# Expert tiles of a fused attention and mixture-of-experts kernel: turned through DRAM by VectorE, with lists of 64-byte entries that each tile gathers itself

## Chip, core and metric

The kernel runs on one core of a Trainium2 chip. The metric is the device time of one execution in microseconds; the figure of a kernel is the median of its runs.

## What is computed

```
scores = z @ z.T / S              # B = 8 batches, S = 2496, z: S x 64
x = u * (relu(scores)**2 @ v)     # u, v: S x 256; 8 * 2496 = 19968 tokens
logits = x @ w_gate               # 256 x 8
e = argmax(logits)                # one expert per token
gate = softmax(logits)[e]
out = gate * (relu(x @ w1[e]) @ w2[e])   # w1: 256 x 1024, w2: 1024 x 256
```

Everything is float32. The kernel gets that accuracy by splitting each operand of a matmul in a high part (rounded to fp32r) and a low part (the rest), and by adding up three products.

## The kernel before

**Attention.** 8 batches of 5 chunks of up to 512 queries, each chunk in 10 steps of 256 keys: 400 steps. `scores` makes a block of squared scores (two matmuls per 128 keys into `ps_s`, Relu and Square on ScalarE, high part `thi`, low part `tlo`); where the block mirrored across the diagonal is there already, it is brought instead: `turn` (L241) transposes 32 x 32 blocks on VectorE and stores 1 MB to the DRAM tile `scr`, and `bring` (L253) reads it back with four DMAs that exchange the blocks. `weighted` (L298) multiplies with v into `acc`. `ready` holds the scores of three steps ahead. SyncE issues all these loads and stores in one queue, in order.

**After each chunk** `gate_x` (L323) makes x of the chunk, transposed, and puts three things in lists of background work, of which one is done in each step: `logits`; `turn_rows`, which writes x as token rows to the DRAM tensor `xrows` (L350); and `route` (L374): choose the expert, then `place`, which counts the token's place in its expert's list with small matmuls. `place` writes the gate beside the row (`xrows` has 272 floats a row: 256 of x, 16 of `gw` whose first is the gate; L429, L431), and scatters the token number, 4 bytes, to its place in the DRAM tensor `lst` by up to four indirect DMAs on GpSimd (L434, 128 tokens each). Unused places of `lst` hold the number of an empty row; `constants` (L205) fills them at the start with six DMAs from GpSimd (L218).

**Expert tiles.** `tile_list` (L444) works out, from the counts, which expert and which part of its list each tile gets: once for six tiles after the seventh batch (list A), and once for the rest after the eighth (list F). It gathers the lists of all tiles in two DMAs (L590), one tile per partition, and `places` (L597) transposes them on TensorE into `idx`, one token per partition. There are 47 tiles in the common path: 31 of four blocks of 128 tokens, 4 of three, 12 of two, mixed so that the two-block tiles are spread out. Two neighbouring tiles can share their weights.

The loop `tiles` (L898) runs over groups, eight in a tile (four in a two-block tile). In a group: `up` (L714) of the group two ahead (matmuls into `ph`, then the high part on ScalarE, L732, and the low part on VectorE, L733), and `down` (L737), which adds into `y`. Around them, at fixed groups:

- first group: `load_w` of the next weights (1 MB each, GpSimd, L639) and `load_x(i + 3)`, one indirect DMA per block, from `xrows` into `rows` (ring of three, L648);
- middle group: `turn_x(i + 2)` (L674). It copies the gates out (L679), cuts the 32-bit values in two 16-bit halves (L689; one half on ScalarE, one on VectorE) into a buffer of the ring `th` (three buffers of 128 x 4 KB), and SyncE transposes each block by a DMA into a second buffer of that ring (L692);
- third group from the end: `split_x(i + 1)` (L695), which joins the halves (L708 on ScalarE, L709 on VectorE) and makes the high part (L710) and the low part (L711). `pinned` (L313) holds it behind what was issued before on each engine;
- `split_piece` (L652) splits a quarter of the weights, two pieces ahead;
- last group: `finish` (L753), which scales with the gate on ScalarE (L760) and VectorE (L761) and scatters the rows to the output on GpSimd (L763).

The first tile is turned differently: copied at `turn_x(0)` (L683) and transposed on TensorE in `split_x(0)` (L704). In the last steps of attention a table `loads` names what is issued for the first tiles: at so many steps before the end `load_x(0)`, `load_w`, `turn_x(0)` and so on; `split_x(0)` stands at the step before the last.

The order of instructions on each engine is made by a scheduler from a model of times; it may put an instruction ahead of others of its engine as soon as its inputs and a buffer are there in that model. It also picks the buffer of a ring. Each engine then executes its own queue in that order.

Of the kernel before, what the change touches and what calls it, by code (L numbers as in the profile page):

```python
# [19 lines left out]
P = 128  # L20
KQ = 64
G, R = 4, 32
D = 256
# [3 lines left out]
ROW = 272  # L27
# [21 lines left out]
def fused_kernel(ctx: ExitStack, tc: tile.TileContext, zt, ut, v, wg, wcat, out):  # L49
# [43 lines left out]
    def ring_rows():  # L93
        return sb.tile([P, QC // P, ROW], F32, name="rows", tag="rows", bufs=3)

# [10 lines left out]
    xrows = dram.tile([NTOK + 1, ROW], F32, name="xrows")  # L106
    lst = dram.tile([NROW + 1, SMALL], F32, name="lst")
# [76 lines left out]
    def iota_i(name, pattern, base=0, mult=0):  # L184
        n = 1
        for _, c in pattern:
# [9 lines left out]
             iota_i("toks", [[S, B], [QC, NC_], [P, QC // P]], mult=1),  # L196
             iota_i("base0", [[CAP, E]]),
             iota_i("pcol", [[0, 1]], mult=2),
             iota_i("tno", [[1, NMAX]])]
    e_down, e_up, toks, base0, pcol, tno = [f for _, f in iotas]  # L200
    base = const.tile([P, E], F32, name="base")
    pads = sb.tile([P, 2, QC], F32, name="x", tag="x")
    padrow, fill = pads[0:1, 0, 0:ROW], pads[:, 1, 0:SMALL]

    def constants():  # L205
# [8 lines left out]
        nc.vector.memset(fill, float(NTOK))  # L214
        nc.gpsimd.dma_start(xrows[NTOK:NTOK + 1, :], padrow)
        for r in range(0, NROW + 1, P):
            m = min(P, NROW + 1 - r)
            nc.gpsimd.dma_start(lst[r:r + m, :], fill[:m])  # L218
# [104 lines left out]
    def gate_x(b, c, acc):  # L323
# [12 lines left out]
        gw = sb.tile([P, QC // P, ROW - D], F32, name="gw", bufs=3)  # L336
        nc.gpsimd.memset(gw, 0.0)
        lw = sb.tile([P, QC // P, R], F32, name="lw", bufs=2)
# [32 lines left out]
    scatters = []  # L371
    lst1 = lst.rearrange("a b -> (a b)").unsqueeze(1)

    def route(t0, n, ns, lw, gw):  # L374

        mlast = n - (ns - 1) * P
        col = (t0 // S * NC_ + t0 % S // QC) * (QC // P)
# [26 lines left out]
        def place():  # L404
# [22 lines left out]
            nf = n // P  # L427
            if nf:
                nc.sync.dma_start(xrows[t0:t0 + nf * P, D:].rearrange("(s p) r -> p s r", p=P), gw[:, 0:nf, :])  # L429
            if mlast < P:  # L430
                nc.sync.dma_start(xrows[t0 + nf * P:t0 + n, D:], gw[:mlast, nf, :])  # L431
            for j in range(ns):
                m = min(P, n - j * P)
                i = nc.gpsimd.indirect_dma_start(  # L434
                    out=lst1, out_offset=bass.IndirectOffsetOnAxis(ap=posi[:m, j:j + 1], axis=0),
                    in_=toks[:m, col + j:col + j + 1], in_offset=None)
                for o in scatters:
                    tc.declare_no_dep(i.ins, o.ins, reason="places are distinct")
                scatters.append(i)
# [4 lines left out]
    def tile_list(nm, nd, nb, n3, ns, done):  # L444
# [6 lines left out]
        kept = ("ndbl", "widx", "idx")  # L451
# [36 lines left out]
        lidx = t("lidx", (P, 2), I32)  # L488
        r["widx"] = t("widx", (P, 2, NT), I32)
        r["idx"] = t("idx", (P, BIG // P, NT), I32)  # L490
# [76 lines left out]
        def rows():  # L567
# [14 lines left out]
            nc.vector.tensor_tensor(lrow, lrow, ident[:, 0:NT], op=ALU.mult)  # L582
            lcol = t("lcol", (P, 1))
            nc.vector.tensor_reduce(lcol, lrow, axis=AX.X, op=ALU.add)
            nc.vector.tensor_copy(lidx[:, 0:1], lcol)
            nc.vector.tensor_scalar(lidx[:, 1:2], lcol, 1.0, float(NROW), op0=ALU.add, op1=ALU.min)
            for h in range(2):
                n = NT if h == 0 else NT - ns
                r["tl", h] = ring_raw().rearrange("p a d -> p (a d)")[:, 0:SMALL]
                nc.gpsimd.indirect_dma_start(out=r["tl", h][:n], out_offset=None, in_=lst,  # L590
                                             in_offset=bass.IndirectOffsetOnAxis(ap=lidx[:n, h:h + 1], axis=0))
# [5 lines left out]
        def places(h):  # L597
            n = NT if h == 0 else NT - ns
            pt = psm.tile([P, QC], F32, name="plt", tag="psm")
            for s in range(SMALL // P):  # L600
                nc.tensor.transpose(pt[:, s * NT:s * NT + n], r["tl", h][:n, s * P:(s + 1) * P], ident[:n, :n])
            for s in range(SMALL // P):
                nc.vector.tensor_copy(r["idx"][:, h * (SMALL // P) + s, 0:n], pt[:, s * NT:s * NT + n])

        return r, [count] + ([middle, others] if ns else []) + [experts, rows] + [nothing] * (6 if ns else 2) + [lambda: places(0), lambda: places(1)]
# [26 lines left out]
    lists, xgs, pieces, turned, gates, xts, yts = {}, {}, {}, {}, {}, {}, {}  # L632
# [9 lines left out]

    def load_x(i):
        which, t, k = order[i]
        src = xrows[0:NTOK - S, :] if which == "A" else xrows
        xg = ring_rows()
        for s in range(k):
            nc.gpsimd.indirect_dma_start(out=xg[:, s, :], out_offset=None, in_=src,  # L648
                                         in_offset=bass.IndirectOffsetOnAxis(ap=lists[which]["idx"][:, s, t:t + 1], axis=0))
        xgs[i] = xg  # L650
# [23 lines left out]
    def turn_x(i):  # L674
# [3 lines left out]
        gates[i] = sb.tile([P, BS], F32, name="gt", bufs=4)  # L678
        nc.vector.tensor_copy(gates[i][:, 0:k], xg[:, 0:k, D])  # L679
        if i == 0:  # L680
            flat = ring_halves().rearrange("p a n -> p (a n)").bitcast(F32)
            turned[i] = flat.rearrange("p (s e) -> p s e", e=D)
            nc.scalar.copy(turned[i].rearrange("p s (i g d) -> p s i g d", i=2, g=G),  # L683
# [132 lines left out]
    for b in range(B):  # L816
        for c in range(NC_):
            s0 = (b * NC_ + c) * NKP
            at(s0 + 2, lambda b=b, c=c: fetch_u(b, c))
            if b == 0:  # L820
                continue
# [161 lines left out]
```

## Time and profile before

| | |
|---|---|
| median of three runs | 2436.0 us (2424.96 to 2438.99) |
| the profiled execution's own time | 2426.16 us |
| its span | 2424.4 us |
| TensorE (PE) busy | 2274.0 us, 94% |
| VectorE (DVE) busy | 1657.8 us, 68% |
| ScalarE (ACT) busy | 1449.8 us, 60% |
| GpSimd (POOL) busy | 635.3 us, 26% |
| mean granted TensorE clock | 0.971 |
| moved by DMA | 383.08 MB, mean 158 GB/s |

How to read the profile: L12 is line 12 of the kernel. PE is the matmuls, PEld the weight loads that overlap them. Names of tiles stand as out<-in, and a `q` behind an engine means its queue alone (waiting or issuing). "Idle before" is the time in which the engine did nothing just before an instruction, and the name behind the arrow is what ended it. The windows view gives busy time in a stretch; the clock in it is the share of full speed that TensorE was granted. The waits view adds up idle time by who waited for whom. Times of DMAs run from issue to landing.

### The profile page before, as it was taken

The numbers are of one execution on the slowest core, as the hardware profiler recorded it, in microseconds if no ns is written. First come the engines' busy times: TensorE is split into PE (matmuls) and PEld (weight loads), VectorE is DVE, ScalarE is ACT, GpSimd is POOL, SyncE is SP. The second block draws the span as 40 slices with busy tenths as digits, with TensorE's granted clock in tenths as the row PEclk, the third lists the DMA queues.
The fourth block names the chain that finished last, engine by engine and source line by source line (L and its number), as shares of the span: only waits on it lengthen the run. The fifth ranks groups of instructions, "written<-read, shape, count | busy, mean of one in ns | idle before, by whom it ended". The sixth has DMA issues, their size and how long they took to land.

```text
span 2424.4 us, 31066 instructions
## 1 busy us (share of the span) xinstructions
PE 2274.0 (94%) x10880; PEld 1886.5 (78%) x10880; DVE 1657.8 (68%) x2895; ACT 1449.8 (60%) x1911; POOL 635.3 (26%) x637
## 2 busy tenths in 40 slices
PE   7999999999989999999999889886988998999998
PEld 4788878887877887878788778775877886888887
DVE  6877878878868878778787666453565564656554
ACT  5758658667657667576586444443554564646554
POOL 3110120120210200201221435433343443345422
PEclk8999999999999999999999989988999998999999
DMA  5777888878988688897787956646364556446430
GB/s 192 183 168 190 170 152 215 161 151 240 142 140 235 138 181 205 135 217 168 161 166 175 219 104 155 128 120 123 108 167 112 172 138 164 117 138 195 146 101 27
DMA packets 305492, 383.08 MB, mean 158 GB/s; under 512 B 209004, under 2 KB 211066, under 8 KB 285872
## 3 DMA queue, kind: packets, MB, share of 16 engines
q1 hardware_dynamic: 273936, 261.93, 51.3%
q0 software_dynamic: 31392, 119.10, 17.2%
q8 instruction: 87, 1.43, 0.3%
q14 instruction: 77, 0.63, 0.1%
HBM read 233.67 MB, written 127.32 MB: 149 GB/s over the span
## 4 chain that ended last, share of the span: by engine, by line
PE 62%; DMA 18%; DVE 7%; SPq 5%; ACT 5%; issue 3%; POOL 1%; ACTq 0%; DVEq 0%; POOLq 0%
PE ph L728 12%; PE acc L309 10%; PE acc L306 10%; PE acc L308 10%; PE y L749 9%; DMA scr<-s 8%; DMA th<-th 6%; PE y L751 4%; PE ps_s L280 3%; PE ps_s L281 3%; DMA s<-scr 3%; SPq L692 2%; SPq L258 2%; DVE t L733 1%; PE pt L357 1%
## 5 line engine op out<-in xcount | busy, mean ns | idle before, releaser
L306 PE MATMUL acc<-thi,t 128*128 128x512 f32 (+1 forms) x1200 | 457.0, 392 | 29.2 <-ACT thi L272 17.7
L309 PE MATMUL acc<-thi,t 128*128 128x512 f32 (+1 forms) x1200 | 464.9, 390 | 1.6 <-POOL t L145 1.6
L308 PE MATMUL acc<-tlo,t 128*128 128x512 f32 (+1 forms) x1144 | 448.5, 392 | 16.3 <-DVE tlo L287 10.3
L749 PE MATMUL y<-t,t 128*128 128x512 f32 x1062 | 389.9, 407 | 47.9 <-ACT t L732 34.4
L728 PE MATMUL ph<-thi,t 128*128 128x512 f32 (+2 forms) x1248 | 378.3, 365 | 15.4 <-DVE t L733 11.1
L282 ACT ACTIVATE tf<-ps_s 128x1024 f32<-128x1024 f32 (+1 forms) x240 | 242.2, 1017 | 220.1 <-PE ps_s L281 211.1
L732 ACT ACTIVATE t<-ph 128x512 fp32r<-128x512 f32 (+1 forms) x328 | 191.8, 589 | 248.6 <-PE ph L728 206.9
L733 DVE SCALAR_TENSOR_TENSOR t<-ph,t 128x512 fp32r<-128x512 f32 (+1 forms) x328 | 219.6, 673 | 176.3 <-ACT t L732 174.7
L751 PE MATMUL y<-t,t 128*128 128x256 f32 x1062 | 293.5, 286 | 5.5 <-DVE t L733 5.3
L306 PEld LDWEIGHTS acc<-thi,t 128*128 128x128 f32 x1200 | 227.5, 190 | 79.4 <-ACT thi L272 21.0
L434 POOL DMA_INDIRECT lst<-toks,posi x160 | 187.3, 1171 | 382.6 <-DMA xrows<-gw 223.9
L749 PEld LDWEIGHTS y<-t,t 128*128 128x128 f32 x1062 | 203.3, 194 | 92.5 <-ACT t L732 36.1
L728 PEld LDWEIGHTS ph<-thi,t 128*128 128x128 f32 x1248 | 227.0, 191 | 56.8 <-DVE t L733 15.3
L308 PEld LDWEIGHTS acc<-tlo,t 128*128 128x128 f32 x1144 | 218.3, 191 | 62.6 <-DVE tlo L287 13.6
L309 PEld LDWEIGHTS acc<-thi,t 128*128 128x128 f32 x1200 | 228.7, 191 | 44.9 <-POOL t L145 3.3
L283 ACT ACTIVATE tf<-tf 128x1024 f32<-128x1024 f32 (+1 forms) x240 | 250.4, 1053 | 4.6
L287 DVE TENSOR_TENSOR tlo<-tf,thi 128x1024 fp32r<-128x1024 f32 (+1 forms) x168 | 203.4, 1214 | 48.0 <-ACT thi L285 47.0
L728 PE MATMUL ph<-tlo,t 128*128 128x512 f32 (+2 forms) x624 | 227.1, 365 | 6.6 <-DVE tlo L711 6.6
L248 DVE STREAM_TRANSPOSE s<-tf 128x1024 f32<-128x1024 f32 x160 | 197.3, 1234 | 48.1 <-ACT tf L283 48.1
L763 POOL DMA_INDIRECT out_dram<-tf,lfidx x136 | 148.3, 1091 | 299.8 <-DVE tf L761 272.7
L751 PEld LDWEIGHTS y<-t,t 128*128 128x128 f32 x1062 | 206.6, 195 | 19.0 <-DVE t L733 8.0
L272 ACT CAST thi<-s 128x1024 fp32r<-128x1024 f32 x104 | 108.7, 1048 | 144.8 <-DMA s<-scr 70.0
(250 smaller groups left out, 4107.4 us busy)
## 6 DMA issues: line engine op xcount, KB each, us to landing
scr<-s SPq DMA_DIRECT2D x80, 1024.0 KB, 8.7
s<-scr SPq DMA_DIRECT2D x320, 256.0 KB, 6.2
vr<-in_v_dram SPq DMA_DIRECT2D x80, 256.0 KB, 6.5
u<-in_ut_dram SPq DMA_DIRECT2D x32, 512.0 KB, 6.4
xrows<-th SPq DMA_DIRECT2D x128, 128.0 KB, 9.4
zr<-in_zt_dram SPq DMA_DIRECT2D x36, 256.0 KB, 6.2
u<-in_ut_dram SPq DMA_DIRECT2D x8, 448.0 KB, 7.0
xrows<-th SPq DMA_DIRECT2D x32, 112.0 KB, 6.8
```

The lines of the kernel that those rows point to most:

```text
L248: nc.vector.transpose(out=to, in_=a.rearrange("p i (t s k) -> p i t s k", t=4, s=G))
L282: nc.scalar.activation(a[:, :, :n], ps[:, :, :n], AF.Relu)
L283: nc.scalar.activation(a[:, :, :n], a[:, :, :n], AF.Square)
L287: nc.vector.tensor_tensor(lo[:, :, :n], a[:, :, :n], hi[:, :, :n].bitcast(F32), op=ALU.subtract)
L306: nc.tensor.matmul(acc[d][:, :n], lhsT=vh, rhs=hi[:, i, :n], start=first and i == 0, stop=False)
L308: nc.tensor.matmul(acc[d][:, :n], lhsT=vh, rhs=lo[:, i, :n], start=False, stop=False)
L309: nc.tensor.matmul(acc[d][:, :n], lhsT=vl, rhs=hi[:, i, :n], start=False, stop=last and i == 1)
L728: nc.tensor.matmul(o, lhsT=w1[:, part, dd, fs], rhs=xx[:, dd, :n], start=p == 0, stop=p == 5)
L732: nc.scalar.activation(hh[:, :m], ph[:, :m], AF.Relu)
L733: nc.vector.scalar_tensor_tensor(hl[:, :m], ph[:, :m], 0.0, hh[:, :m].bitcast(F32), op0=ALU.max, op1=ALU.subtract)
L749: nc.tensor.matmul(y, lhsT=hh[:, cs], rhs=w2[:, f % 2].rearrange("p i d -> p (i d)"), start=f == 0, stop=False)
L751: nc.tensor.matmul(y[:, 0:D], lhsT=hl[:, cs], rhs=w2[:, f % 2, 0, :], start=False, stop=f == NF - 1)
```

## The change

- `xrows` holds 256 floats a row. The gate no longer stands there, and the stores of `gw` go.
- `lst` holds entries of 16 floats (64 bytes): the gate, and the token number as an integer. `place` scatters these entries from `gw`. `lst` grows from 0.66 to 10.5 MB. It is blanked batch by batch: the places that batch b can reach, in two halves, one batch ahead on SyncE's queue (the first batch and the rest on GpSimd at the start).
- `tile_list` no longer gathers and transposes lists. It makes `eidx`, and `load_e(i)` gathers the entries of a tile by one indirect DMA (two in a three-block tile) into `ents`: four neighbouring entries to a partition in a tile of four blocks, two in one of two. `load_e(i + 4)` stands behind `load_x(i + 3)`. `load_x` and `finish` take the token numbers from it, and `finish` the gates.
- `turn_x` is the same for all tiles: one VectorE transpose of 32 x 32 blocks out of `rows` into a buffer of `th`, one store to the DRAM tile `far`, four loads from it into a second buffer of `th`. `split_x` reads that buffer by a rearranged view and makes the high and low part. The cuts, joins, DMA transposes and the TensorE transposes of the first tile go.

```diff
+    def blank(b, h, eng=None):
+        w, n = PAD * ENT, S // PAD // 2
+        at = (b * S + h * S // 2) * ENT
+        i = (eng or nc.sync).dma_start(regions[:, at:at + n * w].rearrange("e (p k) -> p e k", k=w),
+                                       pad[0:n].unsqueeze(1).broadcast_to([n, E, w]))
+        for _, o in scatters:
+            tc.declare_no_dep(i.ins, o.ins, reason="places of another batch")
+        blanks.append((b, i))
...
-            nf = n // P
-            if nf:
-                nc.sync.dma_start(xrows[t0:t0 + nf * P, D:].rearrange("(s p) r -> p s r", p=P), gw[:, 0:nf, :])
-            if mlast < P:
-                nc.sync.dma_start(xrows[t0 + nf * P:t0 + n, D:], gw[:mlast, nf, :])
             for j in range(ns):
                 m = min(P, n - j * P)
                 i = nc.gpsimd.indirect_dma_start(
-                    out=lst1, out_offset=bass.IndirectOffsetOnAxis(ap=posi[:m, j:j + 1], axis=0),
-                    in_=toks[:m, col + j:col + j + 1], in_offset=None)
+                    out=lst, out_offset=bass.IndirectOffsetOnAxis(ap=posi[:m, j:j + 1], axis=0),
+                    in_=gw[:m, j, :], in_offset=None)
...
+    def load_e(i):
+        which, t, k = order[i]
+        en = ents[i] = sb.tile([P, BS, ENT], F32, name="ent", bufs=6)
+        to = en.rearrange("p s w -> p (s w)")
+        eidx = lists[which]["eidx"]
+        parts = [(by4, t, 0, BS)] if k == BS else [(by2, t, 0, 2)]
+        if k == 3:
+            parts.append((lst, eidx.shape[1] - N3 + t - 2 * ND - NB, 2, 3))
+        for src, at, a, z in parts:
+            nc.gpsimd.indirect_dma_start(out=to[:, a * ENT:z * ENT], out_offset=None, in_=src,
+                                         in_offset=bass.IndirectOffsetOnAxis(ap=eidx[:, at:at + 1], axis=0))
...
-        cut, tp = ring_halves(), ring_halves()
-        cut = cut.rearrange("p s (h e) -> p s h e", h=2)
-        for h, copy in ((1, nc.scalar.copy), (0, nc.vector.tensor_copy)):
-            copy(cut[:, 0:k, 1 - h].rearrange("p s (i g d) -> p s i g d", i=2, g=G),
-                 xg[:, 0:k, 0:D].bitcast(U16).rearrange("p s (g i d h) -> p h s i g d", g=G, i=2, h=2)[:, h])
-        for s in range(k):
-            nc.sync.dma_start_transpose(out=tp[:, :, s * P:(s + 1) * P], in_=cut[:, s].rearrange("p h e -> p (h e)"))
+        sq, tp = [ring_halves().rearrange("p a n -> p (a n)").bitcast(F32)[:, 0:k * D] for _ in range(2)]
+        nc.vector.transpose(out=sq.rearrange("p (g i s t) -> p s g i t", g=G, i=2, s=k),
+                            in_=xg[:, 0:k, :].rearrange("p s (g i d) -> p s g i d", g=G, i=2))
+        far = dram.tile([P, F], F32, name="far", tag="far", bufs=4)
+        nc.sync.dma_start(far[:, 0:k * D], sq)
+        for g in range(G):
+            nc.sync.dma_start(tp[g * R:(g + 1) * R].rearrange("p (a e) -> p a e", a=G),
+                              far[:, g * k * 2 * R:(g + 1) * k * 2 * R].rearrange("(a p) e -> p a e", a=G))
         turned[i] = tp
...
+        k = blocks[i]
+        tp = turned.pop(i).rearrange("p (a j t) -> p j a t", a=G, t=R)
+        xh, xl = [x.rearrange("p i n -> p (i n)")[:, 0:k * D] for x in (ring_hi(), ring_lo())]
+        h, l = [x.rearrange("p (j a t) -> p j a t", a=G, t=R) for x in (xh, xl)]
+        nc.scalar.copy(h, tp)
+        nc.vector.tensor_tensor(l, tp, h.bitcast(F32), op=ALU.subtract)
+        xts[i] = [x.rearrange("p (i n) -> p i n", i=2) for x in (xh, xl)]
...
-    loads = {NKP + 3: [lambda: load_x(0)],
+    loads = {NKP + 4: [lambda: load_e(0)],
+             NKP + 3: [lambda: load_e(1)],
+             NKP + 2: [lambda: load_x(0)],
...
                 if i + 3 < hi:
                     load_x(i + 3)
+                if i + 4 < hi:
+                    load_e(i + 4)
```

More of the change, by code (lines that the diff above doesn't have):

```diff
@@ L26 @@
 QC = 512
-ROW = 272
+ENT, PAD = 16, 12
 BIG, SMALL = 512, 256
@@ L104, in slot @@
         return sb.tile([P, 2 * F], F32, name=f"s{i}", tag=f"s{i}")
-    xrows = dram.tile([NTOK + 1, ROW], F32, name="xrows")
-    lst = dram.tile([NROW + 1, SMALL], F32, name="lst")
+    xrows = dram.tile([NTOK + 1, D], F32, name="xrows")
+    lst = dram.tile([(NROW + 2) * SMALL, ENT], F32, name="lst")
     zraw, vraw, ztiles, vtiles, utiles = {}, {}, {}, {}, {}
@@ L580, in rows @@
             nc.vector.tensor_scalar(lrow, lrow, float(NROW), None, op0=ALU.min)
[L582 to L591, printed above, removed]
+            eidx = r["eidx"]
+            for a, z, w in parts + [(nd, 2 * nd, 0)]:
+                if w == 2:
+                    third = t("third", (P, n3))
+                    nc.vector.tensor_scalar(third, lrow[:, a:z], 1.0, float(SMALL), op0=ALU.add, op1=ALU.mult)
+                    nc.vector.tensor_scalar(third, third, prow, None, op0=ALU.add)
+                    nc.vector.tensor_copy(eidx[:, NT:], third)
+                k = 4 if w < 2 else 2
+                nc.vector.tensor_scalar(lrow[:, a:z], lrow[:, a:z], float(SMALL // k), prow, op0=ALU.mult, op1=ALU.add)
+            nc.vector.tensor_copy(eidx[:, 0:NT], lrow)
             nc.vector.tensor_scalar(et, et, float(E - 1), float(2 * P), op0=ALU.min, op1=ALU.mult)
@@ L595, in rows @@
             nc.vector.tensor_scalar(r["widx"][:, 1, :], et, 1.0, None, op0=ALU.add)
[L597 to L605, printed above, removed]
+        return r, [count] + ([middle, others] if ns else []) + [experts, rows]
     NF = F // P
@@ L631, in fused_kernel @@
     piece_of = [NPC * wof[i] + g * fs_of[i] // 2 for i, g in groups]
-    lists, xgs, pieces, turned, gates, xts, yts = {}, {}, {}, {}, {}, {}, {}
+    lists, ents, xgs, pieces, turned, xts, yts = {}, {}, {}, {}, {}, {}, {}
     outs, kept = [], []
@@ L677, in turn_x @@
         xg = xgs.pop(i)
[L678 to L683, printed above, removed]
-                           xg[:, :, 0:D].rearrange("p s (g i d) -> p s i g d", g=G, i=2))
-            return
@@ L819, in fused_kernel @@
             at(s0 + 2, lambda b=b, c=c: fetch_u(b, c))
+            if c == 1 and b + 1 < B:
+                for h in range(2):
+                    at(s0 + 5 + 3 * h, lambda b=b, h=h: blank(b + 1, h))
             if b == 0:
@@ L933, in more @@
         load_w(w, 1)
+        for i in range(lo, min(lo + 4, hi)):
+            load_e(i)
         load_x(lo)
```

74 lines of the change are left out of this document (34 added, 40 removed).

## The prediction

> **What bounds the kernel now.** First the windows view, cut where the attention part ends and the expert tiles begin (last matmul into `acc` at 1398.6 us, first into `ph` at 1398.8). Columns: us, then busy time and instruction count of PE, PEld, DVE, ACT, POOL; granted clock, DMA share, GB/s.
>
> ```profile
> 0.00:1400.00 1400.00, 1344.44 (x6056) 1094.47 (x6057) 1085.67 (x1808) 926.23 (x1007) 239.92 (x261) 0.98 0.82 179
> 1400.00:2424.40 1024.40, 929.58 (x4826) 792.05 (x4824) 572.11 (x1088) 523.59 (x905) 395.39 (x376) 0.95 0.51 129
> ```
>
> PE bounds both parts. In the expert part it stands idle for 1024.4 - 929.6 = 94.8 us; DVE and ACT are busy for little over half. The same view in steps of 50 us shows that the idle time comes in lumps:
>
> ```profile
> 1550.00:1600.00 50.00, 32.93 (x159) 27.45 (x159) 22.20 (x39) 21.20 (x37) 18.93 (x18) 0.80 0.63 120
> 1600.00:1650.00 50.00, 50.00 (x261) 42.46 (x260) 25.82 (x44) 24.46 (x43) 15.47 (x16) 1.00 0.44 121
> 1650.00:1700.00 50.00, 30.67 (x149) 25.65 (x149) 20.57 (x36) 19.72 (x35) 16.36 (x15) 0.80 0.61 109
> ...
> 2400.00:2424.40 24.40, 14.61 (x99) 13.20 (x97) 6.15 (x11) 5.29 (x11) 4.92 (x5) 0.87 0.08 24
> ```
>
> A full window holds 261 matmuls. The window at 1550 holds 159, so it loses (261 - 159)/261 x 50 = 19.5 us, of which 17.1 is idle; the one at 1650 loses 21.5 with 19.3 idle. An idle microsecond thus costs about 1.13, because the granted clock (0.80) is low after it. The last row holds 9.8 us of idle time at the end, which this change leaves alone.
>
> Then the waits of PE from 1400 us on (total, times, longest):
>
> ```profile
> PE y L749 <- ACT t L732: 43.2, 5, 15.9
> PE y L749 <- DVE tf L761: 13.4, 5, 4.4
> PE ph L728 <- DVE t L733: 12.0, 10, 5.1
> PE ph L728 <- DVE tlo L711: 6.6, 5, 1.8
> PE y L751 <- DVE t L733: 5.3, 2, 5.1
> PE ph L728 <- ACT thi L710: 4.1, 5, 1.2
> ```
>
> Together 84.6 us. L732, L733 and L761 are ordinary work on ACT and DVE, so I look at what stands ahead of it there, in the timeline of three places (start, us, instruction, idle time before it and what ended it):
>
> ```profile
> 1413.05 0.69 DVE L689 COPY th<-rows 128x1024 uint16<-128x1024 uint16 x1 [7.26 <-DMA th<-th]
> 1429.68 0.69 DVE L689 COPY th<-rows 128x1024 uint16<-128x1024 uint16 x1 [10.39 <-DMA th<-th]
> 1583.11 0.62 ACT L689 COPY th<-rows 128x512 uint16<-128x512 uint16 x1 [17.14 <-DMA th<-th]
> 1583.15 0.43 DVE L689 COPY th<-rows 128x512 uint16<-128x512 uint16 x1 [18.65 <-DMA th<-th]
> ```
> ```profile
> 1414.63 0.79 PE L749 MATMUL y<-t,t 128*128 128x512 f32 x1 [2.15 <-ACT t L732]
> 1431.03 0.58 PE L751 MATMUL y<-t,t 128*128 128x256 f32 x1 [5.11 <-DVE t L733]
> 1584.80 0.80 PE L749 MATMUL y<-t,t 128*128 128x512 f32 x1 [12.54 <-ACT t L732]
> ```
>
> The cut of a later tile (L689) sits in the in-order queues of ACT and DVE and waits for the DMA transposes of the tile before, which still read the buffer it wants; behind it stand L732 and L733 of the present tile, and PE follows. The first two pairs give the cover: 7.26 - 2.15 and 10.39 - 5.11, so about 5.2 us of such a wait cost nothing. All waits of this kind, and what SyncE's queue waits for ahead of the transposes:
>
> ```profile
> ACT th L689 <- DMA th<-th: 136.7, 37, 20.7
> DVE th L689 <- DMA th<-th: 168.1, 39, 22.4
> SPq L692 <- DVE x L709: 720.3, 43, 38.7
> ```
>
> The last row says that the transposes start when L709 of an earlier tile has freed their target: the x of a tile is turned well ahead, and no tile's own data is late. It is the buffer's hand-over that hurts, and only when the transposes are slow. Issues, with KB and median us to landing, and below them the landing times of all transposes (L692) and of everything written to or read from `scr`:
>
> ```profile
> scr<-s SPq DMA_DIRECT2D x80, 1024.0 KB, 8.7
> s<-scr SPq DMA_DIRECT2D x320, 256.0 KB, 6.2
> th<-th SPq DMA_TRANSPOSE x156, 4.6
> rows<-xrows,lfidx POOLq DMA_INDIRECT x136, 3.1
> ```
> ```profile
> DMA to landing us min/median/max: 2.4/4.6/22.5
> ```
> ```profile
> DMA to landing us min/median/max: 3.4/6.4/26.9
> ```
>
> **The change part by part.** Rows for the instructions concerned (count, busy us, mean ns, idle before):
>
> ```profile
> L248 DVE STREAM_TRANSPOSE s<-tf 128x1024 f32<-128x1024 f32 x160 | 197.3, 1234 | 48.1 <-ACT tf L283 48.1
> L708 ACT COPY x<-th 128x1024 uint16<-128x1024 uint16 (+2 forms) x46 | 54.5, 1186 | 0.0
> L689 ACT COPY th<-rows 128x1024 uint16<-128x1024 uint16 (+2 forms) x46 | 42.2, 916 | 149.3 <-DMA th<-th 136.7 <-DMA out_dram<-tf,lfidx 8.0 <-DMA rows<-xrows,lfidx 4.5
> L709 DVE COPY x<-th 128x1024 uint16<-128x1024 uint16 (+2 forms) x46 | 30.7, 668 | 0.0
> L689 DVE COPY th<-rows 128x1024 uint16<-128x1024 uint16 (+2 forms) x46 | 28.8, 627 | 178.3 <-DMA th<-th 168.1 <-DMA out_dram<-tf,lfidx 9.1 <-DMA rows<-xrows,lfidx 0.9
> L218 POOL DMA_DIRECT2D lst<-x x6 | 3.7, 622 | 0.0
> ```
>
> *Engines.* ACT loses 42.2 + 54.5 = 96.7 us in the expert part and gains nothing. DVE loses 30.7 + 28.8 (and 47 small gate copies) and gains 47 transposes: 31 tiles of four blocks at 1.23, four of three at 0.93, twelve of two at 0.62, together 49 us. Neither bounds the part, so this is worth nothing by itself, with one exception. After a two-block tile the next tile's x is split one group ahead of its first matmul, and the chain L708, L709, L710, L711 is longer than that group. Without the two copies (1.19 + 0.67 us) it should fit: the 6.6 + 4.1 us of PE waiting for L711 and L710 go.
>
> *The hand-over.* The ring `th` keeps three buffers and two uses a tile. The 43.2 + 13.4 + 12.0 + 5.3 = 73.9 us of PE behind L689 remain only as far as the new DVE transpose waits for the store to `far` in the same way. ACT no longer stands in that wait. A store is half of an `scr` store for a full tile (512 KB), in rows of 4 KB; between the lowest 3.4 and the 1 MB median 8.7 I take 7 us, and 6 us for the four loads. Bounds: nothing remains, or all of it does (the same bursts with weights, rows and outputs in flight, where `scr` traffic too has taken up to 26.9). I keep one event of 12.54 and two of about 4, 20 us. The data path gets longer (1.2 + 7 + 6 = 14 us against four issues and 4.6), but the x is turned a tile or more ahead, 1024/47 = 22 us on the mean, so that is covered; without that cover it would cost up to 14 us a tile.
>
> *The lists.* The two list gathers, the PE transposes and the `places` copies go, at no price on the path. Added: 51 gathers of entries, each like L648 about 1.0 us of POOL, 51 us on an engine with 395 of 1024 busy. Each `load_x` stands behind the landing of its own entries (as `rows` 3.1), issued a tile earlier: nothing. But a gather from `lst` waits for the scatters before it (they take 11.0 us to land, row below), and what POOL queues behind (weights, rows, outputs of the first tiles) waits too; up to 11 us, covered by a tile's lead. The first tile is no longer turned on PE: its store and loads take 14 us between `turn_x(0)` and `split_x(0)`, which are four steps of 1400/400 = 3.5 us apart. Between nothing and 13 us; I take 3.
>
> *Attention.* The list is blanked with 64 bytes an entry: 16 DMAs of 104 x 8 x 768 bytes, 10.2 MB, at the part's 179 GB/s 57 us of DMA time, so the share goes from 0.82 to 0.86. They stand on SyncE's queue ahead of the `s<-scr` loads. Gone are 48 small `gw` stores from the same queue. The price shows in what PE already waits for there:
>
> ```profile
> L306 PE MATMUL acc<-thi,t 128*128 128x512 f32 (+1 forms) x1200 | 457.0, 392 | 29.2 <-ACT thi L272 17.7 <-ACT t L143 9.8 <-ACT thi L285 1.6
> L309 PE MATMUL acc<-thi,t 128*128 128x512 f32 (+1 forms) x1200 | 464.9, 390 | 1.6 <-POOL t L145 1.6
> lst<-toks,posi POOLq DMA_INDIRECT x160, 11.0
> ```
>
> Behind L272 it could double (17.7) or shrink a little; I take +4. At the start POOL issues four larger blanking DMAs where six of 0.62 us stood, ahead of L145, which PE waits for: between nothing and some 10 us, I take +2. The scatters write 64 bytes in place of 4, in the same number of pieces: nothing.
>
> *Sum.* Gone: (84.6 - 20) x 1.13 = 73. Added: 4 + 2 + 3 = 9. The span goes from 2424.4 to 2360, and with the 1.8 us around it (2426.2 for the profiled run) to **2362**. The median of the three runs shown is 2436.0, 10 above the profiled run; I leave the forecast where the profiled run puts it.
>
> **The rivals.** *All of it goes.* The store lands early enough at every tile: 84.6 x 1.13 = 96 less 9, so 2339; for it speaks that the longest stalls come only where transposes meet weight loads. *Nothing is won.* In the bursts the store is as late as the transposes were, DVE alone holds PE as before, and only the L710 and L711 waits go, against the 9 added: 2424. For it: `scr` traffic reaches 26.9 us. *Slower.* The scheduler places each DVE transpose too early for a store that lands in 8.7 us, at every tile: beyond the cover of 5.2 us PE loses 3.5 us at 47 tiles, 186 us with the clock, less the 73.9 x 1.13 = 84 it replaces, plus 9: some 2540. It decides from the point where the DVE idle time ahead of the new transpose passes 5.2 us on an ordinary tile. Against it: DVE's present waits are 168.1/39 = 4.3 us on the mean, with ordinary tiles below that.
>
> *A strided DMA is no transpose.* The loads from `far` might fall apart into short strided pieces and outlast a tile's 22 us. Against it stands the `s<-scr` row: the same pattern, runs of a kilobyte and more, 6.2 us. If each tile's four loads took 28 us, 6 us over, 47 x 6 x 1.13 = 319 us come on top: 2680. The Trainium skill, DMA: Bandwidth & Descriptors, section Rules for kernel authors, speaks against this change in that way: transposing in a DMA should use the hardware transpose, and a plain DMA with a rearranged access pattern is put at 19 times its time. By an estimate from that page, 19 times the 4.6 us row, a tile would need 87 us. The trace disagrees where it has the pattern, since the 32 x 32 blocks are turned on DVE and the DMA moves whole rows.
>
> **How the numbers follow.** Forecast 0.55, all goes 0.18, nothing won 0.13, slower 0.12, strided 0.02. 0.5% is 12 us, about what a measurement of this kernel can tell from no change. Faster: the first two and a fifth of the third, 0.76; same: most of the third, 0.10; slower: 0.14. The range takes the first three cases, with the full bounds of the start and of attention: 2318 to 2440.
>
> **What would show it.** Right: no ACT wait on a DMA at the cut, DVE idle ahead of the new transpose mostly under 5 us, windows at 1550 and 1650 with over 245 matmuls, L711's wait gone. Wrong: DVE waits for `far<-th` of 10 us and more, ACT waits at L710 for loads, a lump of idle time near 1400, PE waits behind L272 above 30 us or behind L145 above 5.

## The result, and the profile after

| | before | after |
|---|---|---|
| median (range), us | 2430.48 (2420.09 to 2438.99) | 2304.24 (2301.8 to 2308.67) |
| span of the profiled execution | 2424.4 | 2304.4 |
| last matmul into `acc` starts at | 1398.6 | 1363.6 |
| first matmul into `ph` at | 1398.8 | 1373.2 |
| from there to the end | 1025.6 | 931.2 |

The ratio is 0.9484, 95% interval 0.9439 to 0.953: 126 us faster, where 2362 us had been forecast with a range down to 2318. (One execution of this document, 2344.28 us of the kernel with idle transposes held in place, lay over 1.5% above the fastest of its kernel and is left out.) The spans of the two profiles differ by 120.0 us: attention gives 35.0, the expert part 94.4, and the step between them takes 9.4 back. The forecast had attention 4 us and the start 2 us slower, the first tile 3 us slower and the expert part some 73 us faster: attention went the other way, the expert part and the step went further than it said.

The windows view of after, first the expert part as a whole (from the last `acc` on) and then the two places where the lumps of idle time stood (columns as in the prediction):

```profile
1364.00:2304.40 940.40, 903.01 (x4827) 775.62 (x4825) 570.53 (x1004) 444.10 (x816) 449.14 (x430) 0.99 0.52 164
```
```profile
1550.00:1600.00 50.00, 49.57 (x271) 42.56 (x269) 28.75 (x44) 23.61 (x44) 25.79 (x25) 1.00 0.56 170
1600.00:1650.00 50.00, 49.69 (x252) 42.07 (x253) 29.65 (x46) 22.39 (x40) 24.76 (x25) 1.00 0.60 186
1650.00:1700.00 50.00, 49.69 (x284) 44.19 (x282) 30.73 (x50) 29.18 (x56) 25.41 (x24) 1.00 0.54 159
```

The lumps are gone: the windows at 1550 and 1650 hold 271 and 284 matmuls where they held 159 and 149. What PE still waits for from 1400 us on, and what VectorE and ScalarE wait for at the new turn (waits of after: total, times, longest):

```profile
PE ph L733 <- DVE t L738: 6.0, 5, 3.3
PE y L756 <- DVE t L738: 2.3, 3, 1.8
PE ph L733 <- issue: 1.5, 2, 0.7
PE y L754 <- DVE tf L765: 1.4, 1, 1.4
PE ph L733 <- DVE tlo L716: 0.7, 1, 0.7
PE y L754 <- issue: 0.2, 1, 0.2
```
```profile
DVE th L700 <- DMA rows<-xrows,ent: 16.5, 7, 4.2
ACT thi L715 <- DMA th<-far: 5.7, 1, 5.7
```

12.1 us of 84.6 remain. No turn waits for a store to `far`, and the loads were late once, at the first tile. The attention part, in the windows view of before and then of after:

```profile
100.00:1350.00 1250.00, 1221.94 (x5551) 999.73 (x5549) 980.99 (x1646) 838.93 (x906) 190.91 (x202) 0.99 0.83 175
```
```profile
100.00:1350.00 1250.00, 1245.62 (x5721) 1026.03 (x5720) 1014.04 (x1706) 860.09 (x929) 194.34 (x249) 1.00 0.65 183
```

PE was idle for 28.1 us of this stretch before and for 4.4 after. More bytes per second move (183 against 175 GB/s), and yet the DMA engines are busy for 0.65 of the time in place of 0.83. A byte became cheaper to move; the forecast had the share rise to 0.86. At the start it is the other way (first row before, second after, PE loses 10.7 us):

```profile
0.00:100.00 100.00, 81.86 (x312) 59.59 (x313) 70.12 (x96) 64.30 (x72) 25.20 (x37) 0.93 0.63 195
```
```profile
0.00:100.00 100.00, 71.20 (x248) 50.13 (x249) 55.48 (x66) 57.10 (x64) 23.92 (x39) 0.86 0.92 273
```

### The profile page after: what moved, and what is told of

Read it like the earlier page. It is cut to its first block, busy times and chain, and to the rows that moved or that the text cites. A ratio compares the mean times of both kernels' runs of the same rounds, so it can differ in the third digit from the quotient of the medians.

```text
span 2304.4 us, 31091 instructions
## 1 busy us (share of the span) xinstructions
PE 2233.8 (97%) x10864; PEld 1864.5 (81%) x10864; DVE 1653.1 (72%) x2798; ACT 1368.1 (59%) x1818; POOL 673.9 (29%) x724
## 3 DMA queue, kind: packets, MB, share of 16 engines
q8 instruction: 87, 1.43, 0.3%
## 5 line engine op out<-in xcount | busy, mean ns | idle before, releaser
L445 POOL DMA_INDIRECT lst<-gw,posi x160 | 172.6, 1078 | 963.9 <-DVE posi L442 468.0
L754 PE MATMUL y<-t,t 128*128 128x512 f32 x1062 | 379.3, 397 | 1.7 <-DVE tf L765 1.4
L327 PEld LDWEIGHTS acc<-tlo,t 128*128 128x128 f32 x1144 | 216.7, 189 | 42.9 <-DVE tlo L306 3.5
L754 PEld LDWEIGHTS y<-t,t 128*128 128x128 f32 x1062 | 198.0, 188 | 44.7 <-DVE tf L765 1.8
L767 POOL DMA_INDIRECT out_dram<-tf,ent x160 | 165.6, 1035 | 184.5 <-DVE tf L765 125.0
L756 PEld LDWEIGHTS y<-t,t 128*128 128x128 f32 x1062 | 200.5, 189 | 14.8 <-DVE t L738 3.7
L670 POOL DMA_INDIRECT rows<-xrows,ent x160 | 164.5, 1028 | 107.5 <-DMA ent<-lst,lfeidx 64.9
```

The costliest lines, as they stand in the source:

```text
L327: nc.tensor.matmul(acc[d][:, :n], lhsT=vh, rhs=lo[:, i, :n], start=False, stop=False)
L754: nc.tensor.matmul(y, lhsT=hh[:, cs], rhs=w2[:, f % 2].rearrange("p i d -> p (i d)"), start=f == 0, stop=False)
L756: nc.tensor.matmul(y[:, 0:D], lhsT=hl[:, cs], rhs=w2[:, f % 2, 0, :], start=False, stop=f == NF - 1)
```

## The experiments

"Before" and "after" are the two kernels of this document. Every run was timed beside runs of before on its own chip; before took 2430 to 2473 us there, in the median, so the ratios of different groups differ by more than the changed kernels do. Between groups I therefore compare medians and profiles. That this is fair is not proved, as no changed kernel ran on two chips. It is supported by kernels of different groups that have attention in common: the last matmul into `acc` starts at 1363.6 us in after, at 1364.0 in lists only and at 1362.8 in lists only with its turn held back, and at 1356.3 and 1356.8 in the two kernels with pinned blanks that differ in the turn alone (1349.4 in a third, where one wait took 1.7 us in place of 5 to 6). Line numbers are those of each run's own kernel.

### Which half of the change did it

**Far only**: before with the new `turn_x` and `split_x`, its lists and rows unchanged. **Lists only**: after with the old ones (cuts, DMA transposes, joins). Both are the two hunks of the change's diff in these functions, put in or taken back; far only also keeps the copy of the gates:

```diff
         gates[i] = sb.tile([P, BS], F32, name="gt", bufs=4)
         nc.vector.tensor_copy(gates[i][:, 0:k], xg[:, 0:k, D])
...
+        sq, tp = [ring_halves().rearrange("p a n -> p (a n)").bitcast(F32)[:, 0:k * D] for _ in range(2)]
```

> The kernel before with the new turn through far alone (gates still from the rows, lists and scatters as before). Theory A (in the expert part the DMA transposes hold ACT and DVE up; the attention part gained by the lists): the expert part falls from 1024 to about 930 us, attention still ends near 1398 us, in all 2335 to 2350. Rival B (the expert part gained by the shorter rows and the lists, not by the turn): over 2400. Rival C (the turn gives both parts their gain): attention ends near 1365, in all about 2305.

> The changed kernel with the old turn (cuts, DMA transposes, joins) put back; rows of 1024 bytes, entries and blanks as changed. Theory A: attention ends near 1365 us, the expert part stays above 1000 us, in all 2380 to 2400. Rival B: about 2305 to 2320. Rival C: attention ends near 1398, in all about 2430.

| | median us | ratio (95%) | last `acc` | from there to the end |
|---|---|---|---|---|
| far only | 2331.32 | 0.9565 (0.954 to 0.9591) | 1407.7 | 923.6 |
| lists only | 2418.61 | 0.9929 (0.9901 to 0.9958) | 1364.0 | 1052.0 |

The turn alone is worth 102 us after the last `acc` (1025.8 to 923.6). It gives attention nothing: there the last `acc` came 9 us later, as one wait for `tlo` near the end took 20.2 us in place of 9.7. The lists and rows alone are worth 35 us of attention, but the part behind it grew by 26 us (1025.8 to 1052.0), so that by the medians only 18 us are gained. Both runs missed the times that were expected of the theory (2335 to 2350 and 2380 to 2400); the parts came about as it said, but for these 26 us. They are not all noise: with the new turn, too, the part after the last `acc` is longer with the lists than without (940.9 us in after, 923.6 in far only). Some 6 us of it lie at the very end: from the last scatter's issue to the end of the span it takes 7.2 and 6.9 us in before and far only, and 13.3 in lists only and after. Where the rest comes from was not examined.

In the row of far only, with 4,835 matmuls against 4,826, idle time fell from 94.8 to 23.9 us and busy time from 929.6 to 899.4, the clock rising from 0.95 to 0.99:

```profile
1408.00:2331.30 923.30, 899.40 (x4835) 774.25 (x4834) 575.89 (x1050) 445.89 (x816) 398.17 (x379) 0.99 0.53 167
```

### Attention: which of the small transfers

After with a second scatter added beside each of its own, into a tensor that nobody reads. Three forms: 4 bytes to neighbouring places as in before, 64 bytes, and 4 bytes at places 64 bytes apart.

```diff
+                i = nc.gpsimd.indirect_dma_start(
+                    out=lst4, out_offset=bass.IndirectOffsetOnAxis(ap=posi[:m, j:j + 1], axis=0),
+                    in_=gw[:m, j, 1:2], in_offset=None)
```

The 64-byte form sends `gw[:m, j, :]` to rows of 16 floats; the form apart multiplies `posi` by 16.

> The changed kernel, and besides each scatter of 64-byte entries a scatter of 4 bytes per token to a tensor that nothing reads, with the same places. Theory A1 (scatters of 4 bytes to DRAM held up the other DMAs in attention): stores to scr run above 20 us again once a batch, PE waits behind L291, attention ends 25 to 45 us later, in all 2330 to 2350. Rival A2 (the stores of gw or the row pitch of 1088 bytes did it): 2304 to 2312, the added work of POOL alone.

> Control for the 4-byte scatters: the changed kernel, and besides each scatter a second one of the same 64-byte entries to the same places of a tensor that nothing reads. If it is the size of the pieces that costs: 2304 to 2312, attention ends within 5 us of 1364. If it is the number of scatters or what GpSimd issues: as with the 4-byte scatters, 2325 to 2340.

> As the run with 4-byte scatters beside the entries, but with the 4-byte places 64 bytes apart in a larger tensor (one more VectorE operation and a cast per chunk). If a 4-byte write is slow by itself: as with the dense ones, attention 20 us later, 2325 to 2340. If it is slow because neighbouring tokens are written into the same 64 bytes at nearly the same time: 2306 to 2314.

Then the other two things that went: the stores of `gw` (into a tensor of their own), and the whole old row layout (1088-byte rows, `gw` stored in them, gathers of 1088 bytes).

```diff
+    gwx = dram.tile([NTOK + 1, D + ENT], F32, name="gwx")
...
+                nc.sync.dma_start(gwx[t0:t0 + nf * P, D:].rearrange("(s p) r -> p s r", p=P), gw[:, 0:nf, :])
```
```diff
-    xrows = dram.tile([NTOK + 1, D], F32, name="xrows")
+    xrows = dram.tile([NTOK + 1, D + ENT], F32, name="xrows")
...
+                nc.sync.dma_start(xrows[t0:t0 + nf * P, D:].rearrange("(s p) r -> p s r", p=P), gw[:, 0:nf, :])
```

> The changed kernel, and besides the old 48 stores of 64-byte pieces from gw, at the old row pitch of 1088 bytes, to a tensor that nothing reads. After the run with 4-byte scatters (attention ended 22 us later, 2335 us in all) these stores can have at most the other half of the gain. Theory A1 (scatters of 4 bytes alone): 2304 to 2310, attention ends within 4 us of 1364. Rival A2 (any small write to DRAM holds the others up): attention ends 10 to 25 us later.

> The changed kernel with the old row layout of xrows: 1088 bytes a row, the gw stores in it, and gathers of 1088 bytes; lists, entries and turn as changed. Theory A1: 2304 to 2314. Rival A2 as in the run with gw stores. Rival A3 (rows that begin off a multiple of 256 bytes slow the row stores and the gathers): attention ends 10 to 25 us later and the expert part loses 10 us or more, in all above 2325, while the run with gw stores alone stays at 2310.

The last column counts, in the packet records of the trace, the packets of any queue that took over 1 us between 100 and 1350 us.

| | median us (range) | last `acc` | packets over 1 us |
|---|---|---|---|
| before | 2430.48 | 1398.6 | 1605 |
| after | 2304.24 | 1363.6 | 82 |
| + 4 bytes, neighbouring | 2335.34 (2325.5 to 2342.7) | 1385.6 | 1395 |
| + 64 bytes | 2339.24 (2333.9 to 2341.61) | 1384.7 | 99 |
| + 4 bytes, 64 apart | 2321.82 (2317.11 to 2326.56) | 1369.8 | 89 |
| + `gw` stores | 2304.73 (2303.53 to 2307.44) | 1364.9 | 112 |
| old row layout | 2309.88 (2303.27 to 2313.07) | 1364.0 | 83 |

Stores and row layout cost nothing that shows. The packets single out the 4-byte writes to neighbouring places; neither the size of 4 bytes nor the number of scatters slows them. ScalarE's waits for blocks that are read back from `scr` single them out as well: 70.0 us in before and in far only, 42.9 with neighbouring 4 bytes added, none with 64 bytes or with 4 bytes 64 apart. The times of the kernels do not: 64-byte scatters cost as much, and 4 bytes 64 apart cost 18 us, between the two cases that had been expected. But PE waits for other things there. First the kernel with neighbouring 4 bytes, then the one with 64 (waits of PE, 100 to 1380 us):

```profile
PE acc L327 <- ACT thi L293: 8.0, 4, 3.4
PE acc L329 <- DVE tlo L294: 4.1, 5, 1.1
```
```profile
PE acc L330 <- issue: 3.7, 4, 1.7
PE acc L329 <- issue: 3.6, 3, 1.5
PE acc L327 <- issue: 2.8, 3, 1.5
```

The first are blocks that are read back late from `scr`, as in before (L272 there); the second are waits on nothing that the profile shows, and their cause stayed open. So adding was no clean test, and the last run takes away instead: before, with its own scatters aimed at places 64 bytes apart in a tensor of their own. The lists that the tiles read are preset at the start by eight more small DMAs (not shown).

```diff
+            nc.vector.tensor_scalar(posr, posr, 16.0, None, op0=ALU.mult)
...
-                    out=lst1, out_offset=bass.IndirectOffsetOnAxis(ap=posi[:m, j:j + 1], axis=0),
+                    out=lst4, out_offset=bass.IndirectOffsetOnAxis(ap=posi[:m, j:j + 1], axis=0),
```

> The kernel before, with its 4-byte scatters aimed at places 64 bytes apart in a tensor of their own; the lists that the expert tiles read hold preset token numbers, so the rows they read and write are others than the reference's and only the attention part is to be read. Theory (many 4-byte writes to neighbouring places slow all queues): packets of more than 1 us between 100 and 1350 us fall from 1605 to below 150, scatters land after 3 to 5 us in place of 11, and the last matmul into acc starts at 1350 to 1368 us in place of 1398.6. Rival (another part of the change to rows and lists did it): packets stay above 1000 and the last matmul into acc at 1390 us or later.

The last `acc` came at 1361.8, with 113 packets over 1 us, and ScalarE waited 8.3 us for blocks from `scr`. (The whole run took 2412.15 us, 0.978 with 0.9743 to 0.9817; its expert part is not to be read, as its tiles work on other rows.) The windows view, and from the profile's queue section packets, MB and time of SyncE's queue, first of before and then of this run:

```profile
100.00:1350.00 1250.00, 1245.25 (x5718) 1025.00 (x5717) 1016.79 (x1745) 864.49 (x933) 201.11 (x218) 1.00 0.70 184
```
```profile
q1 hardware_dynamic: 273936, 261.93, 51.3%
```
```profile
q1 hardware_dynamic: 273936, 261.93, 43.2%
```

Same packets, same bytes, a sixth less time (51.3% of 2424.4 us, 43.2% of 2407.9), on a queue that carries none of the scatters. This settles what attention gained: scatters of single 4-byte words, 16 of them in 64 bytes of DRAM, slowed the packets of SyncE's queue (1558 of the 1605 in before are its), and with them the blocks that PE needs from `scr`.

### The start and the first tile

The scheduler had taken the blanks of all batches to the front of SyncE's queue, since nothing they need is ever late. Behind them in the same queue stand loads of v, and matmuls of the first chunk wait for their cast; the longest of these waits ends at 59 us (timeline of SyncE's queue in after, then the waits of after):

```profile
8.96 38.51 SPq L233 DMA_DIRECT2D lst<-pad  x14
```
```profile
PE acc L325 <- ACT t L143: 21.2, 5, 12.7
```

**Pinned**: after, with each blank held in its program place.

```diff
-                    at(s0 + 5 + 3 * h, lambda b=b, h=h: blank(b + 1, h))
+                    at(s0 + 5 + 3 * h, lambda b=b, h=h: pinned(lambda: blank(b + 1, h)))
```

> The changed kernel with the 14 blanks of SyncE's queue held in the place of the program where they are written, so that the scheduler does not put them at the start. If the 35 us that eleven of them hold SyncE's queue at the start cost the 12.7 us wait at 59 us: 2285 to 2292, and no wait of PE above 5 us in the first 100 us. If their bytes cost as much wherever they stand: 2300 to 2306.

2285.51 us (2284.27 to 2288.24), 0.9379 (0.9352 to 0.9405): 19 us below after and, with the next run, the fastest of all. PE is busy for 84.3 of the first 100 us (81.9 in before), its longest wait for that cast there is 4.5 us, and at the first tile it waits 3.4 us in place of 9.2. Of the 19.6 us between the two spans, 7.2 lie ahead of the last `acc` and 5.6 in the step to the first tile; the rest, 6.8, came behind it and was not followed up. **Early**: this kernel with `turn_x(0)` four steps earlier.

```diff
-              NKP - 1: [lambda: load_w(0, 1)],
+              NKP - 1: [lambda: load_w(0, 1), lambda: turn_x(0)],
...
-              NKP - 5: [lambda: turn_x(0), lambda: load_e(2)],
+              NKP - 5: [lambda: load_e(2)],
```

> The kernel with the blanks pinned (2285.5 us), and with the first tile's turn issued four steps of attention earlier. There TensorE still waited 6.15 us at 1353 us and 3.39 us at 1360 us for the first tile's x. Theory (the first tile's store and loads are late because they are issued too late): these two waits fall below 3 us together, and the time is 2274 to 2282 us. Rival (the turn is late because its own rows, or SyncE's queue, come late, wherever it is issued): the waits stay, and the time is 2284 to 2290 us.

2285.46 us (2285.01 to 2287.74), nothing won. The two waits are gone (0.7 us left), but a new one stands 20 us later, where ScalarE stood for 13.72 us (its releaser is not shown) and PE behind it:

```profile
1384.28 0.80 PE L733 MATMUL ph<-thi,t 128*128 128x512 f32 x1 [6.83 <-DVE t L738]
```

So the time was the rival's and the waits were the theory's: a wait moved.

### What the new turn saved

All of the forecast's mechanism rested on slow DMA transposes that hold a buffer. Three things could be the price: the transposes' own lateness, what they do to other transfers, or the place of the cut in the queues. First the transposes alone: the kernel with the blanks pinned, and from the fourth tile on, behind each tile's loads from `far`, the DMA transposes of a constant tile into a buffer that nobody reads. In the first run the scheduler put them into attention, which spoiled it; in the second they are held in place.

```diff
+        for s in range(k):
+            if s % 2 == 0:
+                vt = sb.tile([P, 2, D], F32, name="vr", bufs=4).rearrange("p a n -> p (a n)").bitcast(U16)
+                vt = vt.rearrange("p (a n) -> p a n", a=4)
+            nc.sync.dma_start_transpose(out=vt[:, :, s % 2 * P:(s % 2 + 1) * P], in_=idle_in)
```

> The kernel with the blanks pinned (2285.5 us), and behind each tile's loads from far the DMA transposes of before, of a constant tile into a buffer that nobody reads. They stand beside the same weights, rows and stores but hold no buffer that the turn wants. Theory (DMA transposes slow the 8 KB packets of the other queues, and what waited for them through the buffers of th was the price): packets over 3 us come back (60 to 120, none without), but with far's store and loads still landing in time for most tiles TensorE's idle time in the expert part rises by less than 40 us, and the time is 2290 to 2325 us. Rival (the slowed transfers themselves are the price, whoever waits): the stalls come back in full, the time is 2370 to 2400 us. Third (the transposes were late only by themselves and slow nothing): no packets over 3 us, 2284 to 2290 us.

> The kernel with the blanks pinned (2285.5 us) and the same idle DMA transposes as in the run before, from the fourth tile on, but held in their program place behind each tile's loads from far. Theory (the hand-over through the buffers of th was the price; the transposes also slow other queues' packets, but the rest of the kernel has slack for that): packets over 3 us after 1420 us come back (60 to 100; 0 without), TensorE's idle time after 1406 us rises from 7.8 us to 15 to 35 us, and the time is 2293 to 2320 us. Rival (slowed transfers are the price, whoever waits): idle time after 1406 us of 70 us or more and 2360 to 2390 us. Third (the transposes slow nothing and were only late themselves): no packets over 3 us, 2284 to 2292 us.

Out of place: 2373.28 us, with waits of up to 14.8 us in attention and of 34.4 us at the first tile, whose store stood in SyncE's queue behind ten idle transposes; not to be read as contention. In place: 2320.13 us (2309.44 to 2322.86), 0.9522 (0.9477 to 0.9568), 35 above pinned, with PE's waits after 1399 us adding up to 35.2 us (pinned: 7.8 after 1406), both just over the theory's upper ends. In the packet records the packets over 3 us, from 60 us after the step on, are 95 (pinned 0, lists only 91), all of them 8 KB packets of the GpSimd queue, which brings the weights; the slowest took 8.8 us (pinned 2.3). What is late is not the new turn's own traffic in SyncE's queue: from 1400 us on no split waits for its loads from `far`. VectorE's turn waits for its gathered rows, 53.5 us in all and up to 11.7 at a time (pinned 14.9 and 4.5). So DMA transposes do slow their neighbours, and that is worth up to 35 us, a third of the turn's gain.

Then the buffer: lists only, with four buffers of `th` in place of three (and two of `vr` in place of four, to make room).

```diff
-        return sb.tile([P, 4, QC], U16, name="th", tag="th", bufs=3)
+        return sb.tile([P, 4, QC], U16, name="th", tag="th", bufs=4)
```

> The changed kernel with the old turn by DMA transposes (2418.6 us, 98.4 us of TensorE idle time in its expert part), with four buffers of th in place of three; room for it is made by two buffers of v in place of four, so only the expert part is to be read. Theory (a cut in the queue waits for the transposes of the tile before through the buffer): with one buffer more each cut waits for transposes that were issued half a tile earlier, ACT's and DVE's waits at the cut for DMA th<-th fall from above 100 us each to below 30, and TensorE's idle time in the expert part falls from 98 to 15 to 40 us. Rival (the copies on ScalarE and VectorE and the slowed packets are the price): it stays above 70 us.

2423.71 us (2421.24 to 2439.47), 0.9971 (0.9939 to 1.0003), PE's waits in the expert part 98 to 88 us: the theory fell, in an instructive way. Waits at the cut (L708 in both) from 1400 us on, first lists only, then this run:

```profile
DVE th L708 <- DMA th<-th: 146.6, 36, 12.7
ACT th L708 <- DMA th<-th: 121.5, 34, 13.4
```
```profile
DVE th L708 <- DMA rows<-xrows,ent: 122.3, 31, 9.5
ACT th L708 <- DMA rows<-xrows,ent: 106.0, 31, 8.0
...
DVE th L708 <- DMA th<-th: 52.6, 9, 9.1
...
ACT th L708 <- DMA th<-th: 28.9, 9, 6.3
```

With a buffer free sooner, the scheduler queues the cut sooner, and it waits for its own rows instead. In the median the cut starts 74 us ahead of its tile's low part, against 58 with three buffers. Last, the place: lists only, with `turn_x` of the loop pinned, and the pinned kernel with the same line.

```diff
-                turn_x(i + 2)
+                pinned(lambda: turn_x(i + 2))
```

> The changed kernel with the old turn by DMA transposes (2418.6 us, 98.4 us of TensorE idle time after attention), with turn_x of the loop held in its program place, so that no cut stands ahead of the work of the group before it. With four buffers of th the waits at the cut only moved from the transposes of the tile before to the rows of its own. Theory (the cut is queued before its data and buffer are there, on two engines, and this is two thirds of the price): ACT's and DVE's waits at the cut fall below 40 us each, TensorE's idle time after attention to 25 to 50 us, and the time to 2330 to 2365 us. Rival (copies on ScalarE and slowed packets are the price, wherever the cut stands): idle time above 70 us, time above 2390 us.

> The kernel with the blanks pinned (2285.5 us), with the new turn held in its program place in the same way. Theory (the new turn is queued late enough as it is: DVE waits 15 us for rows at L700): no change, 2281 to 2289 us. Rival (part of the 11 us of idle time left after attention is such waits): 2272 to 2280 us. Third (the place in the program is too late for the store and the loads): TensorE waits at L715 in several tiles, 2295 us or more.

The old turn, held back: 2336.74 us (2328.41 to 2345.39), 0.9486 (0.9434 to 0.9538) where lists only had 0.9929: 82 us less by the medians, with the same copies and the same 156 transposes, and 32 above after. The cut starts 28 us ahead of its low part, and its waits are gone (waits of this run for the transposes, whole span, where L708 is the cut and L727 and L728 are the join; then the longest sums of PE's waits from 1400 us on, which are 25.7 us in all where lists only had 98.4):

```profile
ACT x L727 <- DMA th<-th: 2.2, 1, 2.2
DVE x L728 <- DMA th<-th: 1.4, 1, 1.4
ACT th L708 <- DMA th<-th: 1.2, 1, 1.2
```
```profile
PE y L768 <- issue: 10.7, 5, 3.1
PE ph L747 <- ACT thi L729: 4.5, 5, 1.5
PE ph L747 <- DVE tlo L730: 3.4, 5, 0.8
```

72 packets over 3 us are still there, and hardly anything waits for them. The new turn, held back, took 2300.36 us (2295.76 to 2304.01), by the medians 15 slower than pinned, and 17 in the profiles' part after the last `acc`; the ratios, on two chips, do not show it (0.932 against 0.9379). The time is that of its third case, but the waits are small and at L716 rather than L715: four, of up to 1.9 us, in 16.0 us of PE's waits after 1407 us. Left to the scheduler the new turn starts 55 us ahead of its low part, almost as early as the cut did, but what it waits for is nearly always there: VectorE waits 14.9 us for rows in pinned, where the cut waited above 100 us on each of two engines.

## Why the prediction was wrong

The forecast had a span of 2360 us, and 2304.4 came. Attention with the start was put at +6 and gave -35.0, the expert part was put at -73 and gave -94.4, the step to the first tile was put at +3 and took 9.4. The first of these is 41 of the 56 us that were missed (the second 21, and the third 6 the other way), and none of the rivals had it: the range let the wait behind L272 "shrink a little" at most.

**The scatters, "64 bytes in place of 4, in the same number of pieces: nothing".** This step failed; with it the attention term of +4. Attention ended 35 us earlier, and 42 with the blanks pinned (1356.3 against 1398.6). The old scatters, aimed 64 bytes apart with nothing else of the change, gave 37 (1361.8). The forecast priced what the new operation costs, not what the old one did to others. The profile of before had it in the chain of waits, whose longest pieces (start, us) are these:

```profile
315.33 22.42 DMA scr<-s
657.17 26.93 DMA scr<-s
996.96 22.08 DMA scr<-s
1562.85 20.09 DMA th<-th
1661.70 22.47 DMA th<-th
```

A store with a median of 8.7 us took 22 to 27 three times, and the scatters, of up to 128 small writes each, took 11.0 in the median (3.0 in lists only). I quoted 26.9 as a bound for `far` and 11.0 as a delay, and never asked what made either.

**(84.6 - 20) x 1.13 = 73.** The wait was read rightly: a cut stands in the queue and waits for the transposes of the tile before, and PE behind it. Its reason was not, and two sizes were off. Of 84.6 us, 12.1 remain in after, not 20: a store takes 3.6 us where I took 7, a load 3.0 where I took 6 (issues of far only, KB and median us):

```profile
far<-th SPq DMA_DIRECT2D x31, 512.0 KB, 3.6
th<-far SPq DMA_DIRECT2D x124, 128.0 KB, 3.0
```

And the factor: in far only 70.9 us less idle time went with 30.2 us less busy time, so an idle microsecond cost 1.43, not 1.13. I had counted matmuls against "a full window holds 261", but the full windows of after hold 252 to 284, as their tiles' shapes vary. Busy time and clock of the whole part in one row would have been the better measure.

What I did not separate is why the cut waited. "It is the buffer's hand-over that hurts, and only when the transposes are slow" does not hold: with a fourth buffer PE's waits stayed at 88 us. The place in the queue decided most of it: held back by 30 us, the old turn with the same 156 transposes gives back 82 of the 114 us that lists only stands above after. "ACT no longer stands in that wait" was not the point either, as ACT still makes its copies in the old turn that was held back. The share of slow neighbours (up to 35 us) and that of the place overlap, since late transposes are part of both, so they need not add up.

**Start, +2.** The bounds (nothing to 10) were for GpSimd's blanks; the 14 on SyncE's queue were assumed to stay where the program puts them, "ahead of the `s<-scr` loads". They went to the front: PE lost 10.7 us of busy time in the first 100 us, and pinning them took 19 us off the whole.

**First tile, +3** with bounds 0 to 13: PE waited 9.2 us there, 3.4 with the blanks pinned. Inside its bounds.

**The rivals.** "All of it goes" (2339) was nearest, and far only, without the lists, came close to it: 2331. "Nothing is won", "slower" and "strided" need late stores or loads; no wait for a store stands in after. The lists' own waits came, 64.9 us of GpSimd's in after, and none of PE's remaining waits names them. "Nothing" was still too low for the lists and rows: behind the last `acc`, after takes 17 us more than far only, 5 with the blanks pinned.

Three things stay open: why the lists lengthen the part after attention, with the 6 us at its end; why a second scatter of 64 bytes costs attention 21 us while the packets stay fast; and what the first tile's wait is worth, as it only moved when the turn was issued earlier.

## What to carry to other kernels

Ask of every operation that a change removes what it does to the others: 80 KB of scattered single words cost this kernel's attention some 37 us, and spreading them 64 bytes apart gave it back. Where an instruction waits in an in-order queue, look first at how far ahead of its use it was queued: a line that holds it back was worth 82 us here, one more buffer nothing. It is no rule, as holding back the new turn, which hardly waited, won nothing. The scheduler moved DMAs that depended on nothing to the front of their queue; hold such a DMA where it was meant to be.

## What was not expected of the hardware

- Indirect writes of 4 bytes to neighbouring places slow the packets of SyncE's queue, which carries none of them: 1395 to 1605 packets over 1 us in all queues against 82 to 113 with 64 bytes or with 4 bytes 64 apart. The Trainium skill (DMA: Bandwidth & Descriptors, Specifications) names 512 bytes as the least transfer for line rate, and says that below it the engine reads, modifies and writes. Size below that limit does not explain what these writes do to others: 64-byte writes and 4-byte writes 64 bytes apart, both far below it, leave the packets alone. Of the two spacings that ran, 4 bytes slows them and 64 does not.
- Beside DMA transposes some 8 KB packets of another queue take up to 8.8 us: 95 over 3 us with 148 idle transposes, none without. The Trainium skill (Advanced Engine Details and Errata, X-Bar Transpose (TRN2)) calls transposing DMAs as fast as regular ones. Here the transposes landed after 4.6 us in the median, but up to 22.5 (before), where the plain stores and loads that replace them took 3.7 and 2.9, and at most 12.2 (far only, all tiles), so they were not as fast here.
- Row pitch (1088 or 1024 bytes) and 64-byte stores of `gw` made no difference that can be measured: 2309.9 (2303.3 to 2313.1) and 2304.7 us against 2304.2 (2301.8 to 2308.7).
